# Choosing the PSUM bank of every part in a three-layer kernel, together with its issue order

## The chip, the cores and the metric

The kernel runs on one core of a Trainium2 chip. The metric is the device time of one execution in microseconds (us); lower is better. The core has five engines with queues of their own, each in order: TensorE (PE; its weight loads are shown as PEld), VectorE (DVE), ScalarE (ACT), GpSimd (POOL) and SyncE (SP), which here issues every DMA. TensorE writes its results to PSUM, which the kernel holds as one tile of 8 banks of 512 fp32 columns on 128 partitions; DVE and ACT read them from there.

## The reference, cut to what matters

Three layers follow one another, on 2 batches of 768 positions.

```python
# 1. windowed attention, 8 heads of 64
scores_l = scale * q @ k.T                        # kept where |i - j| < 16
scores_s = scale * q @ k_sum.T + log(32)          # k_sum: maximum over blocks of 32 keys
a = softmax(concat(scores_l, scores_s));  x = a @ concat(v, v_sum)
# 2. four attention experts, the best two of each position weighted by a gate
w = softmax of the top 2 of x @ w_gate
for e in range(4):
    a = softmax(causal(scale * (x @ wq[e]) @ (x @ wk[e]).T))
    out += mask_e * w_e * (a @ (x @ wv[e]) @ wo[e])
# 3. mixer
u = x + ((x.T @ U) @ V).T
result = u + relu(u @ w_ch1) @ w_ch2
```

## The kernel before

**Parts and steps.** The work is cut into 696 parts: the generators `a_scores`, `a_trans`, `qk_proj` and so on, each for one tile. A part runs to its first `yield` in one step, to the next in a second, and so on. Usually the first step issues matmuls, and the later ones read the bank on DVE or ACT and pass it on to POOL. `at` (line 823) registers a part. The loop at line 961 issues one step after the other from a heap, and what decides the order is the table `TIMES` (line 48): `TIMES[u][i]` is the position of step `i` of part `u` among all 1,881 steps. Every engine runs its instructions in this order, so a step that is issued early and waits holds up all that follows on its engine. A dependency, through a buffer or a bank, becomes a semaphore wait between the engines.

**Windowed attention.** 8 pairs of heads, 6 slots of 128 queries each, so 48 slots. `a_scores` (line 348) issues 4 matmuls into 240 columns of a bank; DVE takes the reduce (L358) and ACT the exponentials (L361). `a_trans` (line 363) transposes them, and ACT copies (L368). `a_pv` (line 370) multiplies with the values, two slots into one bank, and DVE scales. `a_out` (line 390) transposes back into the same bank; ACT and DVE split it into a high and a low half. `ksum` and `vsum` make the block summaries, with POOL writing scaled keys (L344) and sums (L206). `fill_k` and `fill_q` (lines 276 and 289) write the constant halves of the operands once, at the start, on POOL, DVE and ACT; `load_q`, `load_k` and `load_v` issue the loads.

**Experts.** 8 pairs of batch and expert. `qk_proj` (line 583) projects queries and keys; ACT and DVE split them, and POOL moves halves (L206). `s_row` (line 610) makes one row block of scores (L621), DVE masks and reduces (L629) and ACT takes exponentials (L632). `s_norm` (line 635) scales on POOL (L645). `t_bank` (line 647) transposes up to 4 blocks (L654), and ACT or DVE (L660, L662) copies. `pv` (line 664) multiplies with the values (L674); ACT and DVE take the sum.

**Mixer.** `c_nat`, `a_mat` and `c_add` add the low-rank term. `w1c` (line 461) multiplies the output projection into the first weight. Then for each batch 32 hidden blocks: `mlp1` (line 775, 6 matmuls, relu on ACT and a low half on DVE) and `mlp2` (line 789, 9 matmuls of 512 columns into three of six accumulators). `resid` (line 796) opens the accumulators, `store` (line 805) copies them out, even tiles on ACT and odd ones on DVE, and issues the store.

**Banks before.** Each kind of work has banks of its own: attention scores 0, 1 and 6 in turn, transposes 2 and 3, values 4 and 5, sums 7. In the experts, rows 4 and 5 span banks 0 and 1, rows 0 to 3 share bank 2 (row 0 at column 256), transposes take 3 and 4, and projections and value products take 7 at first and then 5, 6 and 7 in turn (`ACC`, line 958). In the mixer the six accumulators have banks 2 to 7 in both batches, hidden blocks have 0 and, in the second batch, 0 and 1, and `w1c` has 1.

Of the kernel before, what the change touches and what calls it, by code (L numbers as in the profile page):

```python
# [21 lines left out]
NT = S // 128  # L22
# [13 lines left out]
def f(ap):  # L36
# [131 lines left out]
def tile_block_attention_moe_mixer(ctx: ExitStack, tc: tile.TileContext, qT, kP, vW, vB, wm, woT, wo,  # L168
# [11 lines left out]
    def bank(i):  # L180
        return ps[:, i, :]
# [866 lines left out]
```

## Time and profile before

| | us |
|---|---|
| median of 3 runs | 468.74 (468.25 to 469.14) |
| the profiled execution | 467.39 |
| its span, first to last instruction | 465.6 |
| TensorE busy in the span | 444.1 |
| DVE, ACT, POOL busy | 230.9, 220.9, 177.8 |

The profile shows one execution. "Busy" adds up the time in which at least one instruction of the engine is in flight; matmuls overlap, and their ends are modelled, so a busy TensorE is not one at its peak. In the views of waits, a line reads: waiting engine, what it writes, its line, the arrow, and the engine and line that ended the wait, then us in total, times and the longest. "issue" is a wait that no other engine's event explains. In the views of windows, PE, PEld, DVE, ACT and POOL stand in this order with their busy time and, in brackets, the number of their instructions; then the granted TensorE clock, the DMA share and GB/s. In a timeline row the idle time ahead of it stands in square brackets, with what ended it.

### The profile page before, as it was taken

To read this page: it belongs to the slowest core of one execution; us is meant where nothing else is said; L and a number is where in the kernel's file an instruction comes from. 1 tells how busy PE (TensorE), PEld (TensorE's weight loads), DVE (VectorE), ACT (ScalarE), POOL (GpSimd) and SP (SyncE) were. 2 spreads that over 40 slices of the span, in tenths; PEclk is the share of its full clock that TensorE was granted. 3 is DMA by queue.
4 is the path that set the end of the run, shared out by engine and by line. 5 is a ranking of instruction groups with operands and counts; after the bars stand their busy time and mean duration, and the time that the engine had idled before them with its cause. 6 is when DMAs were issued, how large, how long until landed. Compare 5 with 4: busy or idle time off the path is not lost.

```text
span 465.6 us, 8594 instructions
## 1 busy us (share of the span) xinstructions
PE 444.1 (95%) x3224; PEld 377.9 (81%) x3224; DVE 230.9 (50%) x629; ACT 220.9 (47%) x578; POOL 177.8 (38%) x252
## 2 busy tenths in 40 slices
PE   2999999999999899799999999999999999999996
PEld 1787889978788777576789988988988889888884
DVE  5677765685544776883863545465332011111112
ACT  3677675566745477785744444445332011111111
POOL 7779951465533668981322333435120000000000
PEclk9999999999999999999999999999999999999999
DMA  8976640000000003224053334343103000000003
GB/s 241 265 189 180 171 108 3 1 1 0 2 19 1 1 17 114 92 72 156 3 179 114 114 113 145 127 149 121 48 1 137 0 0 2 0 1 0 1 0 135
DMA packets 14329, 35.19 MB, mean 76 GB/s; under 512 B 1872, under 2 KB 2896, under 8 KB 14288
## 3 DMA queue, kind: packets, MB, share of 16 engines
q1 hardware_dynamic: 14288, 34.65, 24.4%
q8 instruction: 25, 0.41, 0.4%
q14 instruction: 16, 0.13, 0.1%
HBM read 31.50 MB, written 3.15 MB: 74 GB/s over the span
## 4 chain that ended last, share of the span: by engine, by line
PE 91%; DVE 3%; POOL 2%; issue 1%; ACT 1%; DMA 1%; SPq 0%; POOLq 0%; DVEq 0%; ACTq 0%
PE ps L793 28%; PE ps L780 15%; PE ps L590 7%; PE ps L355 5%; PE ps L467 5%; PE ps L674 5%; PE ps L539 4%; PE ps L621 4%; PE ps L801 4%; PE ps L654 4%; PE ps L378 3%; PE ps L366 3%; PE ps L303 2%; PE ps L394 1%; PE ps L702 1%; POOL a L206 1%
## 5 line engine op out<-in xcount | busy, mean ns | idle before, releaser
L787 DVE SCALAR_TENSOR_TENSOR a<-ps,a 128x384 fp32r<-128x384 f32 x64 | 35.2, 556 | 130.6 <-ACT a L785 130.6
L785 ACT ACTIVATE a<-ps 128x384 fp32r<-128x384 f32 x64 | 31.0, 492 | 118.9 <-PE ps L780 99.2
L780 PE MATMUL ps<-x,w1h 128*128 128x384 f32 x256 | 74.6, 338 | 0.0
L793 PE MATMUL ps<-m,a 128*128 128x512 f32 x216 | 52.6, 391 | 0.0
L780 PEld LDWEIGHTS ps<-x,w1h 128*128 128x128 f32 x256 | 47.1, 188 | 2.3 <-ACT x L717 0.4
L793 PEld LDWEIGHTS ps<-m,a 128*128 128x128 f32 x216 | 40.2, 188 | 7.5
L780 PE MATMUL ps<-x,w1l 128*128 128x384 f32 x128 | 43.2, 337 | 0.0
L206 POOL TENSOR_SCALAR a<-a 64x384 fp32r<-64x384 f32 x64 | 32.8, 512 | 20.0 <-ACT a L595 10.7
L590 PE MATMUL ps<-x,m 128*128 128x384 f32 x192 | 37.2, 342 | 0.3 <-DVE c L678 0.3
L590 PEld LDWEIGHTS ps<-x,m 128*128 128x128 f32 x192 | 32.9, 188 | 1.3 <-DVE c L678 0.4
L621 PE MATMUL ps<-a 128*128 128x384 f32 (+4 forms) x128 | 29.5, 342 | 4.2 <-DVE nmx L629 3.7
L645 POOL TENSOR_SCALAR ex<-ex,rs,gate 128x256 f32<-128x256 f32 (+5 forms) x36 | 25.9, 726 | 15.0 <-ACT vb L548 4.8
L227 DVE SCALAR_TENSOR_TENSOR x<-x 128x256 uint32<-128x256 uint32 (+3 forms) x38 | 25.6, 681 | 5.0 <-ACT x L225 4.8
L632 ACT ACTIVATE ex<-ex,nmx 128x256 f32<-128x256 f32 (+5 forms) x36 | 23.4, 654 | 9.5 <-DVE nmx L629 9.3
L629 DVE CUSTOM_DVE_ANT_0 ex<-ps,cc 128x256 f32<-128x256 f32 (+5 forms) x36 | 21.2, 599 | 12.1 <-PE ps L621 8.7
L621 PEld LDWEIGHTS ps<-a 128*128 128x128 f32 x128 | 19.7, 188 | 9.1 <-DVE nmx L629 6.3
L793 PE MATMUL ps<-v,a 128*128 128x512 f32 x108 | 26.6, 395 | 0.0
L793 PE MATMUL ps<-vb,a 128*128 128x512 f32 x108 | 26.5, 392 | 0.0
L780 PEld LDWEIGHTS ps<-x,w1l 128*128 128x128 f32 x128 | 24.0, 188 | 1.9
L793 PEld LDWEIGHTS ps<-v,a 128*128 128x128 f32 x108 | 20.2, 188 | 4.0
L358 DVE TENSOR_REDUCE nmx<-ps 128x2 f32<-128x240 f32 x48 | 19.0, 402 | 8.6 <-PE ps L355 8.4
L662 ACT COPY pt<-ps 128x384 f32<-128x384 f32 (+1 forms) x40 | 20.3, 523 | 6.0 <-PE ps L654 5.7
(215 smaller groups left out, 925.3 us busy)
## 6 DMA issues: line engine op xcount, KB each, us to landing
x<-in_w_dram SPq DMA_DIRECT2D x16, 512.0 KB, 3.6
x<-in_w_dram SPq DMA_DIRECT2D x20, 256.0 KB, 3.1
vb<-in_vW_dram SPq DMA_DIRECT2D x5, 585.0 KB, 6.0
a<-in_kP_dram SPq DMA_DIRECT2D x7, 416.0 KB, 6.0
out_dram<-a SPq DMA_DIRECT2D x10, 256.0 KB, 2.3
x<-in_wm_dram SPq DMA_DIRECT2D x4, 386.0 KB, 6.7
a<-in_w_dram SPq DMA_DIRECT2D x6, 256.0 KB, 3.0
tb<-in_w_dram SPq DMA_DIRECT2D x6, 256.0 KB, 3.3
```

The lines of the kernel that those rows point to most:

```text
L206: pool.tensor_scalar(dst, src, 1.0, 0.0, op0=ALU.mult, op1=ALU.add)
L227: dve.scalar_tensor_tensor(low, high, 3, low, op0=ALU.logical_shift_left, op1=ALU.bitwise_or)
L355: pe.matmul(scb[64 * u:64 * u + 64, hh], QAT[p % NK][hh][:, QT * (2 * t + u):QT * (2 * t + u) + QT], KWT[p % 2][hh][:, 2 * t + u, :], star ...
L467: pe.matmul(acc, wo[k][:, int(a == 2), 128 * c:128 * c + 128], w[k][:, int(a == 1)], start=j == 0, stop=j == 11)
L590: pe.matmul(acc, (WML if wl else WMH)[k][:, 128 * e:128 * e + 128], xt(b, k, xl)[:, c], start=n == 0, stop=n == 11)
L621: pe.matmul(flat[:, base + c0:base + c1], QS[u][:, 128 * i:128 * i + 128], kk[:, c0:c1], start=x == 0, stop=x == 1)
L632: act.activation(ex[:, 0:W], ex[:, 0:W], AF.Exp, bias=nmx, scale=-1.0, accum_out=sums)
L645: pool.tensor_scalar(ex, ex, rs[:, i % 2:i % 2 + 1], gate[b][:, i, e:e + 1], op0=ALU.mult, op1=ALU.mult)
L780: pe.matmul(acc, (W1L if wl else W1H)[ff // 2][:, c, 128 * (ff % 2):128 * (ff % 2) + 128], cp(b, c, xl)[:, o], start=n == 0, stop=n == 5)
L785: act.activation(h, acc, AF.Relu)
L787: dve.scalar_tensor_tensor(l, acc, 0.0, f(h), op0=ALU.max, op1=ALU.subtract)
L793: pe.matmul(outs[3 * j + t], a[:, 128 * t:128 * t + 128], w, start=False, stop=ff == 15 and x == 2, skip_group_check=True)
```

## The change

Two tables are replaced or new. `TIMES` has other positions for nearly all steps. `BANKS` is new and gives the bank of each part, -1 for a part that has none or uses that of another part. `bank(i)` now looks up the bank of the part that is being issued and takes `i` only where there is no table. A value product that uses the bank of its pair's first slot names that part (`pv_part`), and so do `mlp2` and `store` with the part of `resid` that opened the accumulator (`out_part`). Rows 4 and 5 take the named bank and the one after it. Which engine does what, all operands outside PSUM, the shapes and the number of parts stay.

```diff
@@ -46,118 +46,141 @@
-    (66,), (53,), (26,), (1, 2, 3), (9, 14, 22), (0,), (4,), (30,), (6, 31, 40), (11, 15), (10,), (17, 56), (24,),
-    (7,), (13, 20), (18,), (27, 34), (5,), (112,), (175,), (33, 36, 42), (48, 51), (81,), (46, 50, 57), (63, 72),
...
-    (1869, 1873), (1732,), (1866, 1874), (1737,), (1865, 1871), (1748,), (1876, 1880), (1742,), (1875, 1878), (1752,),
-    (1877, 1879),
+    (86,), (13,), (190,), (2, 3, 5), (7, 11, 17), (0,), (4,), (9,), (16, 30, 37), (15, 21), (32,), (26, 52), (8,),
+    (155,), (12, 28), (6,), (63, 67), (19,), (24,), (1,), (39, 41, 46), (54, 58), (105,), (43, 50, 66), (76, 81),
...
+    (1865, 1872), (1742,), (1866, 1871), (1739,), (1867, 1874), (1755,), (1877, 1880), (1758,), (1875, 1878), (1754,),
+    (1876, 1879),
 ]
+BANKS = [
+    -1, -1, -1, -1, -1, -1, -1, -1, -1, -1, -1, -1, -1, -1, -1, -1, -1, -1, -1, -1, 0, 0, 0, 1, 1, -1, -1, 0, 0, 5, 2,
+    2, -1, -1, 4, 1, 1, 3, 7, -1, -1, 1, 2, 4, 4, 4, -1, -1, 6, 2, 2, 7, 3, -1, -1, 3, 5, 0, 7, 3, -1, -1, 0, 3, 6, 7,
+    7, -1, -1, 7, 5, 5, 2, 5, -1, -1, 6, 2, 2, 1, 7, -1, -1, 3, 3, 6, 4, 4, -1, -1, 6, 4, 4, 7, 3, -1, -1, 3, 3, 0, 0,
...
+    -1, 0, -1, 7, -1, 0, -1, 7, -1, 0, -1, 0, -1, 7, -1, 7, -1, 0, -1, 7, -1, 0, -1, 7, -1, 0, -1, 7, -1, 7, -1, 0, -1,
+    7, -1, 7, -1, 0, -1, 7, -1, 7, -1, 0, -1, 7, -1, 0, -1, 0, -1, 6, -1, 3, -1, 1, -1, 4, -1, 2, -1, 5, -1,
@@ -177,8 +200,15 @@
 
     ps = psp.tile([128, 8, 512], F32, name="ps")
 
-    def bank(i):
-        return ps[:, i, :]
+    part_now, pv_part, out_part = [0], {}, {}
+
+    def bank_of(i, part=None, n=1):
+
+        part = part_now[0] if part is None else part
+        return BANKS[part] if BANKS else i
+
+    def bank(i, part=None):
+        return ps[:, bank_of(i, part), :]
 
     def region(tag, n, dt=F32R):
 
@@ -371,7 +401,7 @@
 
         p, t = divmod(s, NSLOT)
         pt = PTT[s % 3]
-        xb = bank(4 + (s // 2) % 2)
+        xb = bank(4 + (s // 2) % 2, pv_part[s // 2])
         for u in range(2):
             for hh in range(2):
                 o = VC * (2 * (s % 2) + hh)
@@ -389,7 +419,7 @@
 
     def a_out(s):
         p, t = divmod(s, NSLOT)
-        x, xb = XQ[s // 2 % 2], bank(4 + (s // 2) % 2)[:, 0:256]
+        x, xb = XQ[s // 2 % 2], bank(4 + (s // 2) % 2, pv_part[s // 2])[:, 0:256]
         for k in range(2):
             pe.transpose(xb[:, 128 * k:128 * k + 128], x[:, 128 * k:128 * k + 128], ident)
         b, pp = divmod(p, NP)
@@ -524,7 +554,7 @@
             CPH[b, c, 0], CPH[b, c, 1] = t[:, 0:S], t[:, S:]
         return CPH[b, c, lo]
 
-    ACC, part_now = {}, [0]
+    ACC = {}
 
     def accbank():
         return bank(ACC[part_now[0]])
@@ -612,9 +642,9 @@
         u = k % 2
         W = 128 * (i + 1)
         if i >= 4:
-            base, parts = 512 - W // 2, [(0, W // 2), (W // 2, W)]
+            base, parts = 512 * bank_of(0, n=2) + 512 - W // 2, [(0, W // 2), (W // 2, W)]
         else:
-            base, parts = 1024 + (256 if i == 0 else 0), [(0, W)]
+            base, parts = 512 * bank_of(2) + (256 if i == 0 else 0), [(0, W)]
         flat = ps.rearrange("p a n -> p (a n)")
         for (c0, c1) in parts:
             for x, kk in enumerate((KH[u], KL[u])):
@@ -786,14 +816,15 @@
         yield Y["rd"]
         dve.scalar_tensor_tensor(l, acc, 0.0, f(h), op0=ALU.max, op1=ALU.subtract)
 
-    def mlp2(b, ff, j, hl, outs):
+    def mlp2(b, ff, j, hl):
         h, l = hl
         for t in range(3):
             for x, (a, w) in enumerate(((h, W2[ff][0]), (l, W2[ff][0]), (h, W2[ff][1]))):
-                pe.matmul(outs[3 * j + t], a[:, 128 * t:128 * t + 128], w, start=False, stop=ff == 15 and x == 2,
+                pe.matmul(out_bank(b, 3 * j + t), a[:, 128 * t:128 * t + 128], w, start=False, stop=ff == 15 and x == 2,
                           skip_group_check=True)
 
-    def resid(b, t, ob):
+    def resid(b, t):
+        ob = out_bank(b, t)
         o = 128 * t
         n = 0
         for c in range(2):
@@ -802,7 +833,8 @@
                           start=n == 0, stop=False, skip_group_check=True)
                 n += 1
 
-    def store(b, t, ob):
+    def store(b, t):
+        ob = out_bank(b, t)
         if b and len(OB) == 3:
             x = region("x00", 2 * S, F32)
             OB[3:] = [f_tail] + [x[:, 512 * i:512 * i + 512] for i in range(2)]
@@ -826,6 +858,7 @@
         if acc:
             accs.append((t, u))
         heapq.heappush(todo, (TIMES[u][0] if TIMES else t, u, 0, fn, args))
+        return u
 
     def A(s):
         return Z["a0"] + Z["pa"] * min(s, 24) + Z["pb"] * max(s - 24, 0)
@@ -849,7 +882,9 @@
     for s in range(NPAIRS * NSLOT):
         at(A(s), a_scores, s)
         at(A(s) + Z["t"], a_trans, s)
-        at(A(s) + Z["v"], a_pv, s)
+        u = at(A(s) + Z["v"], a_pv, s)
+        if s % 2 == 0:
+            pv_part[s // 2] = u
         if s % 2:
             at(A(s) + Z["o"], a_out, s)
     for p in range(NPAIRS):
@@ -928,14 +963,17 @@
                 at(u + Y["wc"] + 1.5 * c, lambda n=n, c=c: w1c(n, c, accbank()[:, 0:256]), acc=True)
             else:
                 at(u + Y["wc"] + 1.5 * c, lambda n=n, c=c: w1c(n, c, bank(1)[:, 256 * c:256 * c + 256]))
-    hl, outs = {}, [bank(2 + t) for t in range(NT)]
+    hl = {}
+
+    def out_bank(b, t):
+        return bank(2 + t, out_part[b, t])
 
     def one(b, ff, j, u):
         acc = bank(u % 2 if b or ff >= LATE_FF else 0)[:, 0:384]
         return mlp1(b, ff, j, u, acc)
 
     def two(b, ff, j):
-        mlp2(b, ff, j, hl.pop((b, ff, j)), outs)
+        mlp2(b, ff, j, hl.pop((b, ff, j)))
 
     for b in range(B):
         P, T = (1.5 * P1, T4 + 48 * P0) if b else (1.5 * P0, T4)
@@ -952,8 +990,8 @@
                 at(t + 0.02, w2_split, ff)
         for i in range(NT):
             j, u = divmod(i, 3)
-            at(T + P * j + Y["rsp"] * u - Y["rs"], resid, b, i, outs[i])
-            at(T + P * (32 if b == 0 else 32 - N_LAST * (1 - j)) + (P * (j - 2) if b == 0 else -P) + Y["sto"] + 0.3 * u, store, b, i, outs[i])
+            out_part[b, i] = at(T + P * j + Y["rsp"] * u - Y["rs"], resid, b, i)
+            at(T + P * (32 if b == 0 else 32 - N_LAST * (1 - j)) + (P * (j - 2) if b == 0 else -P) + Y["sto"] + 0.3 * u, store, b, i)
 
     for i, (t, u) in enumerate(sorted(accs)):
         ACC[u] = 7 if t < A(47) + Z["o"] + 1.6 else 5 + i % 3
```

## Rows read from the trace of the kernel before

**Rows 1.** The page: span, then busy us, share and instructions of each engine.
```profile
span 465.6 us, 8594 instructions
...
PE 444.1 (95%) x3224; PEld 377.9 (81%) x3224; DVE 230.9 (50%) x629; ACT 220.9 (47%) x578; POOL 177.8 (38%) x252
```

**Rows 2.** Windows by stage: us, then busy us and count by engine, clock, DMA.
```profile
0.00:14.80 14.80, 5.54 (x46) 3.04 (x46) 8.25 (x16) 7.28 (x21) 10.86 (x20) 1.00 0.89 248
14.80:90.00 75.20, 75.20 (x1117) 64.60 (x1117) 52.45 (x173) 49.33 (x165) 48.61 (x70) 1.00 0.50 130
90.00:226.00 136.00, 128.33 (x883) 103.23 (x882) 86.98 (x275) 89.04 (x228) 77.76 (x123) 1.00 0.13 41
226.00:461.00 235.00, 235.00 (x1182) 206.99 (x1180) 82.50 (x166) 75.26 (x166) 40.54 (x40) 1.00 0.19 66
```

**Rows 3.** Waits of TensorE matmuls, 90 to 226: total us, times, longest us.
```profile
PE ps L621 <- DVE nmx L629: 3.7, 5, 1.1
PE ps L654 <- POOL ex L645: 0.8, 1, 0.8
PE ps L674 <- ACT pt L662: 0.6, 1, 0.6
PE ps L654 <- DVE pt L660: 0.6, 2, 0.3
PE ps L654 <- POOL vb L645: 0.5, 1, 0.5
PE ps L621 <- POOL a L206: 0.4, 1, 0.4
```

**Rows 4.** Waits of TensorE weight loads (PEld), 90 to 226.
```profile
PEld ps L621 <- DVE nmx L629: 6.3, 8, 1.5
...
PEld ps L654 <- DVE pt L660: 1.9, 6, 0.6
...
PEld ps L654 <- POOL ex L645: 1.7, 3, 0.9
...
PEld ps L674 <- ACT pt L662: 1.1, 1, 1.1
...
PEld ps L621 <- POOL a L206: 0.9, 2, 0.6
...
PEld ps L654 <- POOL vb L645: 0.8, 1, 0.8
```

**Rows 5.** Waits of TensorE weight loads, attention, 14.8 to 90.
```profile
PEld ps L355 <- issue: 3.1, 16, 0.3
```

**Rows 6.** Timeline of the start: start us, us, engine, line, operation, idle before.
```profile
2.83 0.83 POOL L206 TENSOR_SCALAR pt<-cc 64x768 f32<-64x768 f32 x1 [2.39 <-DMA cc<-in_cst_dram]
...
5.51 1.02 POOL L344 TENSOR_SCALAR pt<-a 64x128 f32<-64x128 f32 x2
...
7.77 0.67 PE L355 MATMUL ps<-pt,ex 128*64 128x120 f32 x4 [7.77 <-DMA ex<-in_qT_dram]
...
9.20 1.19 POOL L206 TENSOR_SCALAR w1l<-a 64x1200 f32<-64x1200 f32 x1
...
13.53 0.35 POOL L344 TENSOR_SCALAR c<-ks 64x192 f32<-64x192 f32 x1
...
14.87 0.67 PE L355 MATMUL ps<-pt,ex 128*64 128x120 f32 x4
```

**Rows 7.** Wait instructions on TensorE queue, lines L355 and L366: min/median/max ns, starts.
```profile
L355 PEldq EVENT_SEMAPHORE  x31: 51/51/389, 6.7 to 74.4; - x31
...
L366 PEldq EVENT_SEMAPHORE  x1: 51/51/51, 10.6 to 10.6; - x1
```

**Rows 8.** Windows, the stretch 180 to 210 alone.
```profile
180.00:210.00 30.00, 27.05 (x185) 21.84 (x186) 23.09 (x63) 23.31 (x62) 26.13 (x37) 1.00 0.29 94
```

**Rows 9.** Timeline of the tail: last DVE copy, last store issued.
```profile
461.08 0.69 DVE L813 COPY x<-ps 128x512 f32<-128x512 f32 x1 [0.71 <-PE ps L793]
...
462.19 0.46 SPq L815 DMA_DIRECT2D out_dram<-a  x1
```

More of the change, by code (lines that the diff above doesn't have):

```diff
@@ L48 @@
 TIMES = [
[112 rows of a table removed]
[112 rows of a table added]
+]
+BANKS = [
[21 rows of a table added]
 ]
```

232 rows, old and new, of tables (BANKS, TIMES) are left out of this document.

## The prediction

> **What bounds the kernel now.** I read the page first: TensorE is called busy for 95% of the span and no other engine passes 50% [rows 1]. A busy matmul row is only one in flight, so I cut the span into its four stages. The start (0 to 14.8 us) is more than half empty on TensorE. Windowed attention (14.8 to 90) and the second mixer (226 to 461) show no idle TensorE at all: 75.2 of 75.2 and 235.0 of 235.0. The mixture of experts between them (90 to 226) shows 128.3 of 136.0, so 7.7 us are open idle [rows 2]. The last 4.6 us are the tail.
>
> Next the waits of 90 to 226. On the matmuls' side the largest is a score row (L621) that waits for the reduce (L629) of the scores before it in the same bank: 3.7 us. The transposes (L654) wait 0.6 for the copy L660, again a bank. The rest is late data: normalised scores from POOL (0.8 and 0.5), a copied transpose for the value product (0.6), keys from POOL (0.4). The six kinds come to 6.6 us [rows 3]. On the weight-load side the same six are longer, 12.7 us, because a load that stands still overlaps a matmul still in flight [rows 4]. The array's true loss lies between the two sums; for each kind I take the middle, 9.65 us in all. After the start these waits are what a better order and freer banks can win; matmuls, copies, loads and their shapes stay as they are.
>
> **The change, part by part.** It edits two things: the bank of every part, and the issue position of nearly every step. What is said of the order below is counted from the two position tables: steps sorted by position, and the TensorE parts listed that stand between a part and the one it depends on.
>
> *Score rows and their banks.* Before, rows 4 and 5 of every head share banks 0 and 1, and rows 0 to 3 share bank 2 (row 0 in columns of its own). Of the 48 rows, 3 come straight after the last holder of their columns and 6 with one part between. In the new tables it is 0 and 1. The middle of the wait is 5.0 us [rows 3, 4]; eight of nine close pairs are gone, but the rows still queue on DVE, so I take 80%: **-4.0**.
>
> *Transposes and their banks.* 9 of 48 had one part between them and the last holder of their bank; now none. Middle 1.25 [rows 3, 4], nearly all of it: **-1.1**.
>
> *Data that came late.* From projection to first score row, three of the eight heads had 0, 0 and 1 parts between; now all have 7 or more. From last transpose to value product, 7 of 24 had one part, the median 3; now at least 2, median 10. From last row to first transpose it was 4 to 20, now 7 to 22. The middles are 0.65 for keys, 0.85 for copied transposes and 1.9 for normalised scores [rows 3, 4], 3.4 together. POOL feeds two of the three and is the busiest helper, so again 80%: **-2.7**. The stage gives -7.8. Bounds: all of the load-side sum, -12.7, and 0 if the handovers find other reasons to wait.
>
> *The start.* The fill that the first matmul needs stood third on POOL; now four fills and four key scalings stand before it. With a fill at 0.83 from 2.83 on, the keys' first scalings at 1.02 and the next pair at half of that, it ends at about 8.7, so the first matmul comes 0.9 us later than its 7.77. But TensorE runs without gaps only from 14.87, behind POOL's scaled block sums that end at 13.88. That chain starts behind a fill of 1.19 us which ends at 10.39, and is 3.5 us long [rows 6]. The 1.19 us fill now comes after it, so it starts at about 8.7 and ends at 12.2, 1.7 us earlier. Two loads of expert weights leave the queue's start too, and the first queries go ahead of the first values. Values or DVE may be late next, so I take **-1.2**; bounds -2.5, and +0.9 if the later first matmul passes through.
>
> *Attention.* Nothing to win by the matmul rows. The median count of parts between scores and transpose stays 14, between transpose and value product it goes from 9 to 8. A bank that changes hands between kinds adds a wait on TensorE only where its last reader sits on another engine than the maker of the part's data. Of the 48 transposes, 40 take a bank last read by ACT, which also makes their data, so few waits are new. Scores carry 31 separate wait instructions of 51 ns, transposes 1 [rows 7]. I allow a dozen more: **+0.6**, between 0 and the second rival's price.
>
> *Second mixer.* 235.0 us without a wait [rows 2], the same matmuls, and still at least one whole matmul group between a hidden block and its use. In the first batch the hidden blocks alternate between two banks where one served before, which hides what was hidden: 0, at most 0.5 either way.
>
> *Tail.* Six tiles are stored last. Tile 5's copy on DVE is now issued ahead of tile 3's. Before, DVE's last copy, tile 5's, ran from 461.08 for 0.69; one more behind it ends at 462.46, where the last store was issued at 462.19 [rows 9]. **+0.3**.
>
> Sum: -7.8 - 1.2 + 0.6 + 0.3 = **-8.1 us**. The profiled execution took 467.39 us (465.6 of span and 1.8 around it), so 459.3. The median of the runs, 468.74, lies 1.35 above it; against that I say **460.6 us**.
>
> **A rule against the change.** Scores show what a second wait costs: 31 wait instructions [rows 7], and 16 times the weight load stood still with no named releaser, 3.1 us in all, 0.19 each [rows 5]. The Trainium skill, Perfetto Trace Analysis, section Identifying Dependency Chains, says that an instruction which waits on several engines may get extra semaphore instructions put in front of it. By that rule, on which the trace agrees, any part that takes its bank from another kind could pay, and the second rival's time would be the sum.
>
> **The rivals.** *First, the helpers become the bound.* From 180 to 210 POOL is busy 26.1 of 30 us, ACT 23.3 and DVE 23.1 [rows 8]. If TensorE loses its waits, the same helper work must fit in fewer microseconds; with 3 us less POOL would pass 95%, and normalised scores and keys come late again whatever the bank. For it: the weight splits of the second mixer sit in this stage. Against: over the whole stage POOL has 77.8 of 136 us [rows 2], and the wider spacings let work shift. Half of the stage's gain would stay: 460.6 + 3.9 = 464.5 us.
>
> *Second, slower: waits move into attention.* Its transposes, value products and output transposes are 120 parts with few wait instructions; scores have 31 on 48 parts. At the scores' share they get 78 more. At 51 ns each that costs 4.0 us, at 0.19 each 14.8 [rows 5, 7]. From 0.11 us each they eat the 8.1. At 0.19 the time is 468.74 - 8.1 + 14.8 = 475.4 us. For it: this stage has no idle to spare, so each delay shows. Against: banks pass mostly between parts that ACT reads.
>
> *Third, banks do nothing and the trade is even*: the stage's waits return under other names, about 468.7 us. For it: 39 of 48 rows were already two or more parts apart, and the stage waited all the same. Against: the two bank waits alone are 4.3 us on the matmuls' side [rows 3].
>
> **How the numbers follow.** Forecast (helpers keep up) 0.66, helpers bound 0.17, even 0.06, slower 0.11. Faster is the first two, 0.83. A change under 0.2% (0.9 us) can't be told from none here. The range runs from 454.0, where all load-side waits and the start's best bound are won (468.74 - 12.7 - 2.5 + 0.3), to 467.0, which takes in the helper case with the start at its worst; the even and the slower case, 0.17, lie above it.
>
> **What would show it.** Right: in the stage of experts the rows' wait for the reduce falls under 1 us, the transposes' wait for L660 goes, the stage lasts some 128 us instead of 136, attention and the second mixer keep 75 and 235 us, and TensorE is dense from about 13.5. Helpers bound: the stage still waits for POOL or DVE, with those above 90% busy. Slower: attention grows by several us, with many more wait instructions on transposes and value products. I am wrong if the stage of experts gets shorter by less than 4 us, or if the gain comes from a stage that I called full.

## The result, and the profile after

The changed kernel takes **455.42 us** (454.32 to 456.59, 4 runs) where the kernel before took 468.94 (468.25 to 469.17, 4 runs) beside it. The ratio is 0.971, with an interval from 0.968 to 0.975. Measured once more for the last experiments it was 455.61 against 468.58, 0.973 (0.971 to 0.975). It is faster by 13.5 us; the forecast was 8.1.

The profiled execution took 454.69 us. The page of the changed kernel, span and TensorE (for [rows 1]):

```profile
span 452.9 us, 8633 instructions
...
PE 435.3 (96%) x3224; PEld 377.5 (83%) x3224; DVE 227.9 (50%) x629; ACT 218.3 (48%) x578; POOL 179.1 (40%) x252
```

Its windows by stage (columns as in [rows 2]; each stage begins at about the same work, but the counts show that some 20 matmuls changed sides between attention and experts):

```profile
0.00:15.40 15.40, 4.54 (x44) 2.94 (x45) 7.59 (x14) 5.83 (x19) 12.56 (x23) 1.00 0.87 219
15.40:88.00 72.60, 72.52 (x1102) 62.60 (x1104) 50.16 (x168) 49.86 (x165) 46.86 (x68) 1.00 0.52 139
88.00:214.00 126.00, 124.02 (x904) 105.69 (x899) 90.23 (x285) 89.23 (x232) 81.68 (x125) 1.00 0.16 54
214.00:448.40 234.40, 234.24 (x1181) 206.30 (x1180) 78.66 (x163) 73.37 (x163) 38.01 (x38) 1.00 0.18 60
```

The start is 0.6 us longer than in [rows 2], attention and the second mixer are as full as they were. The stage of experts takes 126.0 us instead of 136.0, and TensorE stands idle in it for 2.0 us instead of 7.7. The waits that are left in it on the matmuls, and the three longest on the weight loads (for [rows 3, 4]):

```profile
PE ps L651 <- POOL a L236: 1.4, 1, 1.4
PE ps L704 <- DVE nmx L659: 0.6, 1, 0.6
```

```profile
PEld ps L704 <- issue: 2.0, 9, 0.4
PEld ps L651 <- POOL a L236: 1.7, 1, 1.7
PEld ps L704 <- DVE nmx L659: 1.1, 2, 0.9
```

The rows' wait for the reduce (3.7 and 6.3 us before) is gone, the transposes' wait for their copy too. One wait grew: a row (L651) waits for keys from POOL, 1.4 us on the matmuls and 1.7 on the loads, where it was 0.4 and 0.9 before. One value product (L704) waits 0.6 us for a bank that a row's reduce (L659) has just read.

The idle of the matmul rows shrank by 5.7 us, though, and the time by more than twice that. To see the rest I cut both spans at the same work: from the third slot's first scores, where TensorE becomes dense, to the first matmul that opens an output accumulator. But for a handful the same matmuls lie between them (2,006 and 2,001 records). First the kernel before, then the changed one (stretch, then PE, PEld, DVE, ACT, POOL as in [rows 2]):

```profile
14.87:227.46 212.59, 204.92 (x2006) 168.98 (x2005) 140.83 (x449) 139.79 (x395) 126.33 (x192) 1.00 0.26 72
```

```profile
15.40:214.02 198.62, 196.55 (x2001) 168.29 (x2001) 140.41 (x452) 139.09 (x397) 128.54 (x192) 1.00 0.29 85
```

The stretch is 14.0 us shorter. Of that, 5.6 us are idle between matmul rows (7.7 to 2.1) and 8.4 us came out of "busy" matmul time (204.9 to 196.6). So matmul rows count as busy while they, or the loads ahead of them, wait. The weight loads' busy time hardly moves (169.0 and 168.3); their **idle time fell from 43.6 to 30.3 us, by 13.3**, which is nearly the whole gain. So of the two sides of the waits it is the loads' side that shows what TensorE lost. Since the loads' busy time is the same, that idle time is what is left of the length, and its change, not its size, is the gain: 30.3 us of it remain. Nearly all of it went behind the first score row of the experts, 32.8 to 19.7; in front of that row it was 10.8 and is 10.6:

```profile
92.31:227.46 135.15, 127.48 (x866) 102.39 (x863) 86.62 (x269) 88.81 (x225) 76.37 (x120) 1.00 0.13 41
```

```profile
90.65:214.02 123.37, 121.39 (x863) 103.68 (x862) 88.22 (x277) 87.10 (x225) 80.60 (x122) 1.00 0.17 55
```

Outside the stretch nothing was gained: it begins at 15.40 instead of 14.87, the rest up to the last matmul takes 234.3 instead of 233.6, and the tail 4.5 both times.

### The profile page after: what moved, and what is told of

The parts are those of the page before. It is cut to its first block, busy times and chain, and to the rows that moved or that the text cites. A ratio compares the mean times of both kernels' runs of the same rounds, so it can differ in the third digit from the quotient of the medians.

```text
span 452.9 us, 8633 instructions
## 1 busy us (share of the span) xinstructions
PE 435.3 (96%) x3224; PEld 377.5 (83%) x3224; DVE 227.9 (50%) x629; ACT 218.3 (48%) x578; POOL 179.1 (40%) x252
## 4 chain that ended last, share of the span: by engine, by line
PE 92%; POOL 2%; DMA 2%; DVE 1%; SPq 1%; issue 0%; ACT 0%; DVEq 0%; POOLq 0%; ACTq 0%
PE ps L823 29%; PE ps L810 15%; PE ps L620 7%; PE ps L497 5%; PE ps L385 5%; PE ps L704 4%; PE ps L651 4%; PE ps L569 4%; PE ps L832 4%; PE ps L684 3%; PE ps L408 3%; PE ps L396 3%; PE ps L333 2%; DMA vb<-in_vW_dram 2%; PE ps L424 1%; PE ps L732 1%
## 5 line engine op out<-in xcount | busy, mean ns | idle before, releaser
L815 ACT ACTIVATE a<-ps 128x384 fp32r<-128x384 f32 x64 | 31.2, 490 | 117.6 <-PE ps L810 62.6
L810 PE MATMUL ps<-x,w1h 128*128 128x384 f32 x256 | 73.5, 337 | 0.1
L651 PE MATMUL ps<-a 128*128 128x384 f32 (+4 forms) x128 | 28.0, 338 | 1.4 <-POOL a L236 1.4
L257 DVE SCALAR_TENSOR_TENSOR x<-x 128x256 uint32<-128x256 uint32 (+3 forms) x38 | 23.0, 610 | 5.3 <-ACT x L255 5.1
L659 DVE CUSTOM_DVE_ANT_0 ex<-ps,cc 128x512 f32<-128x512 f32 (+5 forms) x36 | 21.1, 597 | 9.1 <-PE ps L651 4.6
L662 ACT ACTIVATE ex<-ex,nmx 128x512 f32<-128x512 f32 (+5 forms) x36 | 23.3, 647 | 3.4 <-DVE nmx L659 3.1
L823 PEld LDWEIGHTS ps<-vb,a 128*128 128x128 f32 x108 | 20.1, 188 | 3.7
L651 PEld LDWEIGHTS ps<-a 128*128 128x128 f32 x128 | 19.9, 189 | 3.5 <-POOL a L236 1.7
```

The lines of the kernel that those rows point to most:

```text
L257: dve.scalar_tensor_tensor(low, high, 3, low, op0=ALU.logical_shift_left, op1=ALU.bitwise_or)
L651: pe.matmul(flat[:, base + c0:base + c1], QS[u][:, 128 * i:128 * i + 128], kk[:, c0:c1], start=x == 0, stop=x == 1)
L662: act.activation(ex[:, 0:W], ex[:, 0:W], AF.Exp, bias=nmx, scale=-1.0, accum_out=sums)
L810: pe.matmul(acc, (W1L if wl else W1H)[ff // 2][:, c, 128 * (ff % 2):128 * (ff % 2) + 128], cp(b, c, xl)[:, o], start=n == 0, stop=n == 5)
L815: act.activation(h, acc, AF.Relu)
L823: pe.matmul(out_bank(b, 3 * j + t), a[:, 128 * t:128 * t + 128], w, start=False, stop=ff == 15 and x == 2, skip_group_check=True)
```

## The experiments

All are edits of the two tables; the program around them is that of the changed kernel. "Stretch" is the one just defined, "loads idle" its length less PEld's busy time, both of the profiled execution; one execution differs from another, as the changed kernel's two rows show (198.6 and 200.0). Lines of the experiments are one lower than the changed kernel's (L650 is its L651).

| run | order | banks in the experts | median us | ratio to before | stretch | loads idle |
|---|---|---|---|---|---|---|
| before | old | by kind | 468.3 to 468.9 | 1 | 212.6 | 43.6 |
| changed | new | of the change | 455.42 | 0.971 (0.968 to 0.975) | 198.6 | 30.3 |
| 1 | old | free | 468.77 | 1.002 (1.000 to 1.003) | 212.6 | 43.5 |
| 2 | old, early projections | by kind | 488.42 | 1.041 (1.039 to 1.044) | 231.0 | 57.3 |
| 3 | old, early projections | free | 485.20 | 1.036 (1.034 to 1.038) | 229.4 | 55.1 |
| 4 | new | free, close handovers | 463.49 | 0.990 (0.988 to 0.992) | 207.5 | 38.8 |
| 5 | new, early read-outs | by kind | 469.29 | 1.003 (1.001 to 1.006) | 212.3 | 43.9 |
| 10 | new, early read-outs | by kind | 468.10 | 1.000 (0.998 to 1.001) | 211.1 | 42.9 |
| 11 | new, early read-outs | of the change | 456.24 | 0.974 (0.972 to 0.977) | 201.2 | 32.5 |
| 9 | the change again | of the change | 455.61 | 0.973 (0.971 to 0.975) | 200.0 | 31.1 |
| 6 | new, old start | of the change, but for 42 parts of attention | 458.56 | 0.979 (0.977 to 0.982) | 203.2 | 34.2 |
| 7 | new, keys first | of the change | 459.28 | 0.981 (0.979 to 0.983) | 202.8 | 33.2 |
| 8 | new | free, wide handovers | 457.80 | 0.978 (0.975 to 0.980) | 202.3 | 33.8 |
| 12 | new, one split later | of the change | 454.11 | 0.970 (0.968 to 0.972) | 198.4 | 30.3 |

**Run 1: the banks alone.** The old `TIMES`; of `BANKS` the experts' parts. For the fourth expert (rows 5 to 0, transposes, value products):

```diff
-rows 0 0 2 2 2 2   transposes 3 4 3 3 4 3   value products 6 5 7
+rows 2 1 7 1 0 5   transposes 7 3 5 0 2 0   value products 5 1 6
```

> Banks alone: the issue order of the kernel before, step by step; only the score rows, transposes, value products and projections of the experts' stage take other banks, chosen so that almost no part follows the last holder of its bank closely (scores, output tiles and hidden blocks keep the old banks). If the bank waits are the loss (my theory), the rows' wait for the reduce (3.7 us on matmuls, 6.3 on loads) and the transposes' wait for the copy (0.6 and 1.9) go: 4 to 8 us faster than the kernel before, about 462. If the order alone makes the gain (rival), the time stays at that of the kernel before within 1 us, and the waits come back as late data (keys, normalised scores). If banks and order pay only together, 0 to 2 us faster.

Nothing was gained: 468.77 us, and 43.5 us of idle loads as before. The waits of TensorE's matmuls show why:

```profile
PE ps L650 <- POOL a L235: 1.4, 1, 1.4
PE ps L650 <- DVE nmx L658: 1.4, 2, 0.9
PE ps L683 <- DVE sums L668: 1.4, 1, 1.4
PE ps L650 <- ACT pt L691: 1.0, 1, 1.0
...
PE ps L683 <- ACT pt L691: 0.7, 1, 0.7
PE ps L703 <- ACT pt L691: 0.6, 1, 0.6
```

The rows' wait for the reduce (L658) fell from 3.7 to 1.4 us, and in its place stand late keys (1.4), a transpose that waits behind the sums of the normalising step on DVE (1.4), value products for copied transposes (0.6), and a row and a transpose that wait for a bank which ACT has yet to copy out (1.0 and 0.7). The loads' side shows the exchange more clearly:

```profile
PEld ps L650 <- POOL a L235: 3.0, 4, 1.6
PEld ps L683 <- POOL ex L674: 2.7, 4, 1.5
PEld ps L703 <- ACT pt L691: 2.3, 4, 1.1
...
PEld ps L650 <- DVE nmx L658: 1.1, 1, 1.1
```

The waits for banks fell from 8.2 us to 3.4 (1.1 here, 1.5 and 0.8 for ACT's copies), and those for late data (keys, normalised scores, copied transposes) rose from 4.5 to 8.9. TensorE came out of the bank's wait sooner and ran into that of the data. The bank had held back work whose data was no earlier. This is one table of banks; that no other one would pay in the old order is not shown.

**Runs 2 and 3: one part of the new order alone.** The fourth expert's projections in run 2 (positions of their steps):

```diff
-qk_proj 0,3  (783, 793, 808, 811, 814, 818, 820), (815, 823, 828, 830, 831, 835, 841)
+qk_proj 0,3  (753, 770, 785, 796, 797, 809, 810), (798, 811, 816, 817, 818, 822, 823)
```

> One part of the new order alone: in the old order with the old kinds of banks, each expert's projection of queries and keys (second half of the second expert, both halves of the third to eighth) starts 5 us of TensorE work earlier, so that 2.9 us or more lie between it and the first score row (0 to 2 before for three heads). By the waits named in the trace keys are late for 0.4 us on matmuls and 0.9 on loads: 0.5 to 1 us faster. If waits are mostly put down to the wrong releaser and late keys are the larger loss, 4 us or more faster, and the rows' wait for the reduce shrinks although the banks stay.

> Both of the above: old order with early projections and freed banks in the experts' stage. If the two losses are separate, the gains of the two runs add up (5 to 9 us faster, about 461); if they are one loss under two names, it gains no more than the better of the two. What still lies between this and the changed kernel (455.4) is the rest of the new order.

Neither theory had it: 20 and 17 us slower. Matmul waits of run 2:

```profile
PE ps L650 <- DVE nmx L658: 11.1, 8, 3.1
PE ps L683 <- POOL vb L674: 2.2, 2, 1.1
...
PE ps L703 <- ACT pt L691: 1.2, 1, 1.2
```

The rows' wait for the reduce is 11.1 us, three times that of before. The step moved is half a head's projection, 12 matmuls that take 2.26 us on TensorE (before, from 129.92 on) and do not wait for scores; in the old order it stood where scores wait for the reduce and the normalising step. Moved away, it left that wait bare. That three heads had no part or one between projection and first row was no loss but the price of a cover elsewhere. With free banks (run 3) the same loss has other names: 8.9 us for normalised scores from POOL (L683), 3.3 for copies. A part of the loss is the clock, which the last section shows.

**Run 4: the new order with close handovers.** Positions as in the changed kernel. Banks of 83 parts differ, so that in all they follow the last holder's read-out as closely as before; fourth expert:

```diff
-rows 1 2 5 6 6 1   transposes 6 7 6 0 7 6   value products 1 3 6
+rows 0 1 6 5 7 3   transposes 4 4 7 0 2 6   value products 2 1 3
```

> The new order, step by step; only the banks of rows, transposes, value products and projections in the experts' stage are chosen again, this time so that as many parts as possible follow the last holder of their bank closely (as closely in all as in the kernel before). If bank waits are the loss, 4 to 8 us slower than the changed kernel, about 461, with rows waiting for the reduce again. If the order makes the gain, it stays at about 455.4.

463.49 us, 8 us slower than the changed kernel with the same order: so here the banks do count. The loads' waits (columns as in [rows 4]):

```profile
PEld ps L703 <- DVE nmx L658: 2.2, 4, 0.9
PEld ps L683 <- ACT pt L691: 1.7, 4, 0.6
```

The first line is a value product that waits for a row's reduce, which has nothing to do with its data: a wait across kinds, which free banks make possible and a bad table makes real.

**Runs 5, 10 and 11: the new order with bound banks.** For the third to seventh expert the banks go by kind again. The new order starts a part while the only bank of its kind is held; there the holder's read-out is drawn forward, ahead of the next part's first step:

```diff
-s_row 6,4  (1046, 1059, 1077)  bank 2      s_row 6,5  (1050, 1055, 1065)  bank 0
+s_row 6,4  (1047, 1050, 1077)  bank 0      s_row 6,5  (1051, 1056, 1065)  bank 0
```

> The new order of TensorE's work, unchanged, but for the third to the seventh expert the banks are bound to kinds again as in the kernel before (rows 4 and 5 in banks 0 and 1, rows 0 to 3 in bank 2, transposes in 3 and 4, the rest in 5 to 7). The new order starts a part while an earlier one of its kind still holds the only bank, in 18 places; there the read-out of the earlier part is issued ahead of the later part's first matmul. If the new order wins because it keeps more parts in flight, which bound banks don't allow (the theory left by the first four runs), most of the gain of these five experts is lost: 461 to 466 us. If the order of TensorE's work is what counts and the banks only have to be free of close handovers by chance, it stays within 3 us of the changed kernel's 455.4.

> As in the fifth run, with six score rows fewer bound, so that no buffer in SBUF is written ahead of its reader: 24 of the 30 score rows of the third to seventh expert, and their transposes, value products and projections, have the banks of their kinds again; 13 parts of those before a shared bank are read out ahead of their place (18 steps moved), TensorE's order is the new one. If parts in flight make the gain: 463 to 470 us. If the order of TensorE's work alone makes it: within 3 us of the changed kernel.

> The control for the run before: the same 18 read-outs drawn forward on DVE and ACT, but the banks of the changed kernel. If the bound banks are what costs, it stays within 2 us of the changed kernel. If the in-order queues of DVE and ACT are what costs (a read-out that waits for its matmul holds back what stands behind it), it takes the same time as the run before.

Run 5 took 469.29 us; in it the reduces of two score rows (row 2 of the second expert, row 3 of the sixth) write their buffer in SBUF before its reader has read it, so some exponentials are others, with all instructions kept. Run 10, without those, takes 468.10: **the whole gain is gone**, although TensorE's order is the new one. (Counted again, 16 parts, not 13, are read out early.) Run 11 has the same steps in the same places and the banks of the change: 456.24. So the read-outs' places on DVE and ACT cost nothing that can be measured, and the bound banks cost 11.9 us. The same waits in run 10 and in run 11:

```profile
PE ps L650 <- DVE nmx L658: 5.6, 7, 1.1
PE ps L683 <- DVE nmx L658: 2.1, 2, 1.0
PE ps L683 <- ACT pt L691: 1.2, 3, 0.5
```

```profile
PE ps L650 <- POOL a L235: 0.7, 1, 0.7
PE ps L703 <- DVE nmx L658: 0.6, 1, 0.6
```

What the new order asks of the banks can be counted in the tables. From a part's first matmul to the place of its last read-out, weighed by TensorE's work in between (an estimate, with matmul durations from the trace of before), the experts hold 3.2 of the 8 banks in the old order, 5.3 in the new one and 4.4 in run 10. Run 11 has the steps of run 10, so the same count, and loses nothing: so it is not the number of banks held that costs, but that a part has to take the one that its kind names. In run 10 six score rows come straight behind the last holder of their columns, in the kernel before three, in the changed kernel none. That the new order needs the room of two more banks fits the count, but no run shows it by itself.

**Run 9** is the control beside runs 10 to 12.

> The changed kernel itself, beside the next three. Three small edits of it came out 2 to 4 us above its 455.4, each for another reason. If that is their doing, it gives 455 to 456 here too. If it is the execution (the values' landing at the start, the spread of 2.3 us of its four runs), it gives 457 to 458, and small edits can't be told from none.

It agrees with the first measurement, and its interval lies clear of those of runs 6 and 7 and just clear of run 8's, so their 2 to 4 us are their edits' doing.

**Run 6: the old start.**

```diff
-load_k 0, fill_q 0,1, load_q 0, fill_q 1,0, ksum 0, load_q 0, fill_k 0,1, ksum 0, fill_k 0,0, load_v 0, ...
+load_k 0, fill_q 1,1, load_v 0, fill_q 2,0, ksum 0, load_q 0, fill_q 0,0, fill_k 0,0, ksum 0, fill_k 0,1, ...
```

> The steps ahead of the fourth slot's scores in the order of the kernel before (first fill third on POOL, the first loads in their old places), the rest in the new order. The changed kernel's first matmul comes at 9.23 us and the fourth slot's scores at 15.40, against 7.77 and 14.87 before. If the new start costs what these rows say, 0.5 us faster than the changed kernel (about 454.9), with the fourth slot at 14.9. If the forecast of the start was right and only the landing of the values varies from one execution to the next, it is the same or up to 1 us slower.

It is slower by 3 us, where 0.5 us of gain was expected. (The rows at 15.40 and 14.87 are those of the third slot, not of the fourth.) The edit also gives 42 parts of attention, up to the seventeenth slot's scores, other banks than the change has. Two of the waits on TensorE up to 92 us, in an execution that is the slowest of the six (460.91; the median is 458.56):

```profile
PE ps L332 <- DMA w1l<-in_vW_dram: 1.3, 1, 1.3
PE ps L332 <- DMA vb<-in_vW_dram: 1.2, 1, 1.2
```

and SP's timeline, of run 6, of the changed kernel and of the kernel before (start, duration of the issue, line, operation):

```profile
5.85 1.37 SPq L514 DMA_DIRECT2D x<-in_wm_dram  x2
...
16.14 0.43 SPq L324 DMA_DIRECT2D w1l<-in_vW_dram  x1
```

```profile
13.99 0.43 SPq L325 DMA_DIRECT2D w1l<-in_vW_dram  x1
```

```profile
14.19 0.43 SPq L295 DMA_DIRECT2D w1l<-in_vW_dram  x1
```

The old start issues two loads of the experts' weights (L514) at 5.85, ahead of what the first pairs still need; the values of the third pair go out at 16.14 instead of 13.99, and TensorE waits 1.3 us for them. But the kernel before has the same two early loads, issues those values at 14.19 and does not wait. So the trace of this one execution suggests that the new start buys the loads behind the first matmul, and not that matmul; whether the 3 us are the start's, or in part those of the other banks, is not shown.

**Run 7: keys ahead of weight splits.** The largest wait left is at 183 us: a row waits 1.4 us (its load 1.66) for the eighth expert's key copies on POOL, behind two weight splits.

```diff
-w1_split 0,0 (.., 1101)  w1_split 0,1 (.., 1119)  qk_proj 1,3,0 (.., 1108, 1115, 1123, 1129)  qk_proj 1,3,1 (.., 1111)
+w1_split 0,0 (.., 1106)  w1_split 0,1 (.., 1121)  qk_proj 1,3,0 (.., 1101, 1103, 1104, 1105)  qk_proj 1,3,1 (.., 1102)
```

> The changed kernel with five of the eighth expert's key copies on POOL issued ahead of two weight splits (0.75 us each), which stand between them in the table. The largest wait of the experts' stage, 1.66 us at 183 us of a score row for POOL's key copy, should lose about 1.5 us: 454.0 us if TensorE's next wait does not take it over; the same time (455.4) if another late part stands right behind it.

The wait went, and a longer one came, 3.7 us slower in all. Three engines' timelines show the chain, POOL, DVE and TensorE:

```profile
177.31 5.00 POOL L235 TENSOR_SCALAR a<-a 64x384 fp32r<-64x384 f32 x8
182.39 2.14 POOL L265 TENSOR_TENSOR x<-x,x 128x256 fp32r<-128x256 f32 x3
```

```profile
186.34 0.32 DVE L252 TENSOR_SCALAR x<-x 128x256 uint32<-128x256 uint32 x1 [3.48 <-DMA x<-in_w_dram]
...
187.14 0.96 DVE L658 CUSTOM_DVE_ANT_0 vb<-ps,cc 128x768 f32<-128x768 f32 x1
```

```profile
188.16 1.02 PE L650 MATMUL ps<-a 128*128 128x320 f32 x6 [3.08 <-DVE nmx L658]
```

The keys run through at 177.31, the splits come after them at 182.39. But the first split also frees the buffer of the next weight load. That load goes out at 183.16, where the changed kernel sends it at 179.12; DVE's first step on it waits 3.48 us for the transfer, and the reduce that stands behind it on DVE starts at 187.14; the row that needs that reduce's bank waits 3.08 us.

**Run 12: only the second split later.** The next load's buffer stays on time.

```diff
-w1_split 0,1  (1087, 1092, 1098, 1114, 1119)
+w1_split 0,1  (1087, 1092, 1098, 1114, 1129)
```

> The seventh run moved five key copies ahead of two weight splits, and a weight load that needs the first split's buffer came late. Here only the second split goes behind the last key copy; the first, and the load behind it, keep their places. POOL's last key copy should end 0.75 us earlier, and the wait at 183 us fall from 1.66 to 0.9: 0.5 to 0.8 us faster than the changed kernel beside it. If a load or another queue is late again, no gain, and the wait has a new name.

```profile
182.29 0.80 PE L650 MATMUL ps<-a 128*128 128x384 f32 x3 [0.42 <-POOL a L235]
```

The row's wait is 0.42 us, where it was 1.39 and, in run 9, 1.25; the experts, from first row to first open accumulator, take 122.8 us instead of 123.3 in run 9. At 454.11 us (454.06 to 456.10) it is the fastest of all, but its interval and that of run 9 overlap: the wait is shown to be shorter, the time is not shown to be.

**Run 8: wide handovers.**

```diff
-rows 1 2 5 6 6 1   transposes 6 7 6 0 7 6   value products 1 3 6
+rows 1 2 6 5 0 4   transposes 2 4 1 0 1 7   value products 2 0 5
```

> The new order, step by step; in the experts' stage the banks are chosen again so that a part follows the last holder of its bank by half a microsecond more than the holder's read-out needs, where it can (the shortfalls in all go from 5.4 to 2.4 us by a count of TensorE's work). If bank handovers still cost something in the changed kernel, 0.5 to 1.5 us faster, and the 0.7 us wait of a value product for a row's reduce at 180 us goes. If they are used up, the same time as the changed kernel within 0.5 us.

457.80 us, 2 us slower. The table is better by the count it was made with and worse on the chip; the loads' idle is 33.8 us instead of about 31, spread over many small waits. Counting TensorE's work between two holders doesn't see when DVE and ACT really come to read. I found no single wait that explains it, and it stays open.

## Why the prediction was right, and where it was not

The forecast was faster by 8.1 us; it is 13.5, inside the range. Its mechanism stands in the main: the stage and the bank waits that it named are where the gain is. Two things in it do not: the terms do not add, and one wait that it called won grew.

- **Score rows and banks, -4.0, transposes and banks, -1.1, late data, -2.7.** The stage of experts gave nearly everything, as the prediction said: of the 14.0 us over the stretch from the dense start, for which the sum had 7.2 (-7.8 and +0.6 for attention), 13.1 are loads' idle behind the first score row. The rows' wait for the reduce and the transposes' for their copy are gone whole. Of the late data the copied transposes and the normalised scores are nearly gone (on the loads 1.1 to 0.2 and 2.5 to 0.4), but the keys' wait grew (0.9 to 1.7), so by the prediction's own middles the late data gave some 1.6 us and not 2.7. The term was mis-sized at the step "the array's true loss lies between the two sums; for each kind I take the middle". The loads' side was the loss: its idle fell by 13.3 us, and the low end of the range, which took that side in full (12.7), was the better estimate. In part that is luck: the six kinds named gave 10.4 of their 12.7 us on that side, and the rest came from small waits that the prediction did not list. The discount of a fifth was not needed for the rows, and for the late data it was too small. (The terms of that low end add up to 453.8, not 454.0.)
- **The terms are not separate.** The prediction priced the banks and the data as two gains that add. Run 1 has the first alone and is worth 0; run 10 has the order, with most of the experts' banks bound again, and is worth 0; together they are worth 13. The third rival, that a bank's wait returns under another name, is right for banks alone. The prediction also counted close pairs of projection and first row as loss; runs 2 and 3 show that they were a cover.
- **The start, -1.2.** Wrong in sign in the row (+0.5, 14.87 to 15.40), and too small to be read there: in run 9 the same kernel has the third slot at 14.48. Its step "values or DVE may be late next" is what happened. The product that sums the values' blocks (L333) waited for their load, 1.15 us in the first execution and 0.24 in run 9:

```profile
9.23 0.67 PE L385 MATMUL ps<-pt,ex 128*64 128x120 f32 x4 [9.23 <-DVE pt L368]
...
12.25 1.51 PE L333 MATMUL ps<-vb,cc 96*32 96x128 f32 x24 [1.15 <-DMA vb<-in_vW_dram]
...
15.40 0.67 PE L385 MATMUL ps<-pt,ex 128*64 128x120 f32 x4 [0.48 <-DVE vs L343]
```

```profile
11.33 1.51 PE L332 MATMUL ps<-vb,cc 96*32 96x128 f32 x24 [0.24 <-DMA vb<-in_vW_dram]
...
14.48 0.67 PE L384 MATMUL ps<-pt,ex 128*64 128x120 f32 x4 [0.48 <-DVE vs L342]
```

  The first matmul came at 9.23, 1.5 us later than before and not 0.9, because the fill that it needs took 1.27 us on POOL where 0.83 was taken from [rows 6]. What the start is worth stays open: run 6 loses 3 us without it, but has other banks in attention too.
- **Attention, +0.6, and the slower rival.** Neither: TensorE's queue carries 24 separate wait instructions in this stage where it had 43; scores have none (31 in [rows 7]), transposes 12 of 51 ns each. The loads' idle share is 13.8% (72.6 us, of which 62.6 busy) after 14.1% in [rows 2]. The rival's price of 0.19 us fails too: without one wait instruction the scores' loads still stand 12 times for no named releaser, as long in all as the 16 times of [rows 5], so those stops were not what a wait instruction costs. In the stage of experts the wait instructions did become more, 29 on rows, transposes and value products where there were 20.

```profile
PEld ps L385 <- issue: 3.0, 12, 0.9
```

- **Helpers as the bound.** From 150 to 180 us POOL is busy 27.3 of 30, above the 90% that the prediction gave as the sign; TensorE's matmuls waited for it once, 1.4 us at 183. Runs 7 and 12 show that this one wait is a matter of two instructions' places.
- **Second mixer 0, tail +0.3.** The mixer takes 0.7 us more, a little over the 0.5 allowed; why is not shown. The tail's order changed as read: the last copy is tile 3's, and the last store goes out 1.35 us after the last matmul's end at 448.36, 0.2 later than before. It did not reach the end: the tail is 4.5 us both times.

```profile
449.00 0.68 DVE L845 COPY a<-ps 128x512 f32<-128x512 f32 x1
449.71 0.33 SPq L847 DMA_DIRECT2D out_dram<-a  x1
```

The Trainium skill, Perfetto Trace Analysis, section Matmul Optimizations, asks that all eight banks be put to use so that instructions can overlap. The runs agree with half of it. The kernel before already uses all eight in the experts, each for its kind; to free them of kinds is worth 0 in the old order (1.002) and 11.9 us in the new one (runs 10 and 11). Banks give room; the order has to use it.

## What to carry to other kernels

A buffer that is bound to one kind of work limits the order, not only the waits that carry its name: where a wait for a buffer is the longest in the list, ask what would be late right behind it, and change order and binding together or not at all. To size what TensorE loses, compare the weight loads' idle time over a stretch of the same work; the matmul rows' idle showed 5.6 of 14 us here. Its change between two orders is the measure; how much of it can be won, its size does not say. A piece of work that waits for nothing is a cover: before it is moved, look at what stands bare without it, and before a step on a helper is moved back, look for the load that waits for its buffer.

## What the hardware showed that was not expected

In these runs a long wait was paid twice. In run 2 a row waited 3.08 us, from 168.4 to 171.5; the windows of the wait and behind it (granted TensorE clock third from the right):

```profile
168.00:171.50 3.50, 0.42 (x5) 0.18 (x3) 3.28 (x14) 0.91 (x4) 1.55 (x4) 0.99 0.00 0
171.50:173.00 1.50, 1.50 (x6) 1.46 (x7) 0.06 (x1) 1.03 (x2) 0.00 (x0) 0.50 0.00 0
173.00:175.00 2.00, 1.40 (x5) 0.68 (x3) 1.62 (x8) 1.19 (x4) 0.00 (x0) 0.53 0.00 0
175.00:177.00 2.00, 1.37 (x10) 0.78 (x10) 1.04 (x5) 1.35 (x4) 1.67 (x2) 1.00 0.00 0
```

In the two windows behind the wait the granted clock is 0.50 and 0.53, that is its lower level of 1.2 GHz: the four matmuls of 128x320 from 171.47 on take 1.44 us, where four of them took 0.85 at 125.45 at a clock of 1.00. From 175 on it is full again. The same follows the wait of 2.07 us that ends at 116.5 (0.50 from 118 to 120), and in run 7 that of 3.08 us (0.50 from 190 to 192); behind the changed kernel's longest wait, 1.4 us up to 183.2, the clock stays at 1.00. Over the stretch of run 2 the mean is 0.96, and its loads' busy time is 173.8 us instead of 169.0. The matmuls of the kernel before had no wait above 1.1 us in this stage, and its clock stays at 1.00 there [rows 2], so an edit of the order can cost more than the waits in its list say.
